# Loading a small decay vector through another engine's queue, and a new order of two early attention steps, in a fused attention and MLP kernel

## The chip, the cores and the metric

The kernel runs on one core of one Trainium2 chip. The metric is the device time of one execution in microseconds (us). A profile gives the span of one execution, from the first to the last instruction; the device time is about 1.8 us longer than the span. The experiments ran on three chips (e and g on one, f on another, h1 on a third), each with the kernel before beside it, so kernels of different letters are compared by their ratios to before.

In the profile PE is TensorE's matmuls, PEld its weight loads, DVE is VectorE, ACT is ScalarE, POOL is GpSimd, and SP is SyncE, whose work here is to issue transfers (SPq). ACTq is a transfer issued by ScalarE. PSUM is the memory that TensorE writes its results to; to evacuate a result is to copy it from there. A load has landed when all of its 16 completions have come.

## The reference

Decayed causal attention in blocks of 64 rows, then a two-layer MLP on its output.

```python
# q, k, v: (4 batches, 8 heads, 768 rows, 64);  lam: 8 decays, one per head
for b in range(nb):                                    # 12 blocks of 64 rows
    intra = einsum('bhic,bhjc->bhij', qb, kb) * Dmask  # lam ** (i - j), causal
    intra = einsum('bhij,bhjd->bhid', intra, vb)
    inter = einsum('bhid,bhde->bhie', qb * lam ** (pos + 1), kv_state)
    out[block] = intra + inter
    kv_state = lam ** 64 * kv_state + einsum('bhsd,bhse->bhde', kb * lam ** (63 - pos), vb)
x = out as (3072, 512)
result = gelu_tanh(x @ w_in) @ w_out                   # w_in 512 x 2048, w_out 2048 x 512
```

## The kernel before

The attention is cut into 24 steps, each of one batch, 256 rows and four of the eight heads. Steps 0 to 3 give the first 512 rows of x, and these start the MLP: its first group of work, `Hps = w_in . x` with GELU, then fills TensorE between the later attention steps. Every q, k, v and weight tile is loaded through SyncE's queue, in this order, with lam in front:

```python
    lam_bc = const.tile([P, H], FP32)
    pin(nc.sync.dma_start(out=lam_bc[:], in_=lam.unsqueeze(0).to_broadcast([P, H])))
    for s in range(4):
        load_step(s)                       # q, k, v of a step: three transfers of 256 KB
    for j in range(4):
        for part in ((0, 1) if j < 2 else (None,)):
            load_win(j, part)
    for j in (0, 2, 1, 3):
        load_wout(j)
    for s in range(4, 9):
        load_step(s)
```

One step passes through these stages: `prep` (q times a power of lam on VectorE, for step 3 on GpSimd; k cast on ScalarE, v on GpSimd), `stage_t` (eight transposes on TensorE into PSUM, then an evacuation), `scores`, `causal` (VectorE multiplies the scores by the mask, 1.22 us), `products` (the key product and the value product into the two PSUM banks OK), `update` (VectorE adds the key product to the running state, "t"; GpSimd spreads it, "u"), and `x_out` (ScalarE evacuates x, two pieces of 0.38 us each). The order of these calls is the program order on every engine. The order of before from step 2 on:

```python
    update(1, 0)
    idle(3)                                # three filler matmuls
    scores(2)
    products(2, None)
    causal(2)
    prep_v(3)
    update(2, 0)
    update(1, 1)
    update(2, 1, "t")
    idle(2)
    stage_t(3)
    OK1 = products(None, 1, evacuate=False)[0]
    OK2 = products(None, 2, evacuate=False)[0]
    x_out(2, OK2)
    x_out(1, OK1)
    scores(3)
    banks = products(3, None)
    update(3, 0)
    c01, c23 = slice(0, 2), slice(2, 4)
    cast_win(0, 0, 256, 128, c01)
    cast_win(0, 256, 512, 256, c01, on_act=True)
    causal(3)
    queue_group(0)
    fill(4)                                # fill(n): the next n pieces of MLP work
    products(None, 3, banks)
    ...                                    # cut
    # later, before step 4:
    cast_wout(0, (POOL, POOL))
    for m in W_SUMS:                       # five sums of w_out parts on VectorE
        sum_wout(0, m, DVE)
    fill(8)
    cast_wout(2, (ACT, ACT))
    cast_wout(1, (POOL, ACT))
    cast_wout(3, (POOL, ACT))
    fill(9)
    prep(4)
    stage_t(4)
```

## Time and profile before

| | before |
|---|---|
| device time, median of 3 runs | 206.26 us (206.10 to 206.67) |
| span of the profiled execution | 204.3 us |
| PE busy | 196.8 us (96%) |
| VectorE, ScalarE, GpSimd busy | 71%, 53%, 34% |

TensorE is busy for 96% of the span. Of the 7.5 us that it does not work, 3.7 are in the first 20 us, where the attention steps wait for loads and for each other, and 3.8 follow the last matmul (200.53), while the result leaves the core. The lines of the slices, the chain and the timeline of this kernel stand in the prediction below, each with what it shows.

### The profile page before, as it was taken

What the parts mean: (1) busy time and instruction counts of PE and PEld (TensorE: products, weight loads), DVE (VectorE), ACT (ScalarE), POOL (GpSimd) and SP (SyncE); (2) the same over time, 40 slices, a digit from 0 to 9 for tenths busy, and PEclk for the clock granted to TensorE, in tenths of its full rate; (3) what the DMA queues carried; (4) which work ended last, traced back from release to release, by engine and by line L of the source; (5) the groups of instructions that cost most, each with busy time, mean ns of one, the idle gap of its engine ahead of it and who ended that gap; (6) DMA issues with size and microseconds to landing.
All of it is one profiled execution on the core that took longest, in us unless ns stands there. A gap on an engine that the chain in (4) does not pass through costs nothing.

```text
span 204.3 us, 5584 instructions
## 1 busy us (share of the span) xinstructions
PE 196.8 (96%) x2321; PEld 127.6 (62%) x2321; DVE 144.8 (71%) x271; ACT 107.7 (53%) x204; POOL 70.1 (34%) x80
## 2 busy tenths in 40 slices
PE   7888999999999999999999999999999999999992
PEld 2454644456875788654688654788554788545881
DVE  4887627867599999929997828996739673136552
ACT  2364678475683573477722477641576331577110
POOL 5595123646487750436134404314412100000000
PEclk9999999999999999999999999999999999999999
DMA  4999999999999999996449993647330003300014
GB/s 132 299 321 385 387 388 379 285 291 315 297 262 228 296 241 173 235 285 176 91 128 266 181 279 94 152 107 156 75 85 0 0 3 103 107 0 0 3 51 156
DMA packets 64074, 37.86 MB, mean 185 GB/s; under 512 B 17712, under 2 KB 59184, under 8 KB 64048
## 3 DMA queue, kind: packets, MB, share of 16 engines
q1 hardware_dynamic: 63760, 37.24, 68.1%
q8 instruction: 18, 0.29, 0.6%
q10 hardware_dynamic: 288, 0.26, 0.4%
q14 instruction: 8, 0.07, 0.1%
HBM read 27.27 MB, written 6.29 MB: 164 GB/s over the span
## 4 chain that ended last, share of the span: by engine, by line
PE 89%; DMA 3%; SPq 2%; ACT 1%; DVE 1%; issue 1%
PE Hps L401 37%; PE O2ps L416 10%; PE MB L470 8%; PE MA L470 7%; PE MD L470 7%; PE Sps L271 4%; PE MC L470 4%; PE Hps L515 4%; PE OK L329 3%; PE OK L320 3%; DMA k<-in_k_dram 3%; SPq L68 2%; PE OK L306 1%; PE Tps L242 1%; DVE t L366 1%
## 5 line engine op out<-in xcount | busy, mean ns | idle before, releaser
L401 PE MATMUL Hps<-xT,w_in 128*128 128x512 f16 (+1 forms) x416 | 79.1, 346 | 0.0
L405 ACT ACTIVATE gT<-Hps 128x512 f16<-128x512 f32 x88 | 52.1, 598 | 21.9 <-PE Hps L401 21.1
L401 PEld LDWEIGHTS <-w_in 128*128 128x128 f16 x416 | 40.2, 98 | 33.5
L373 POOL TENSOR_TENSOR u<-t,lumask 128x256 f16<-128x256 f32 x40 | 31.4, 792 | 80.6 <-DVE t L366 58.4
L446 DVE TENSOR_TENSOR gs<-gT 128x512 f16<-128x512 f16 (+1 forms) x70 | 36.6, 586 | 10.8 <-ACT gT L405 10.6
L280 DVE TENSOR_TENSOR PT<-Sps,mask 128x1024 f16<-128x1024 f32 x24 | 29.2, 1216 | 17.1 <-PE Sps L271 17.1
L470 PEld LDWEIGHTS <-gs 128*128 128x128 f16 x360 | 34.9, 98 | 4.0
L211 POOL TENSOR_TENSOR v<-v,dv 128x512 f16<-128x512 f32 x24 | 29.2, 1220 | 4.9 <-DMA v<-in_v_dram 4.8
L343 ACT ACTIVATE xT<-OK 128x256 f16<-128x256 f32 x48 | 18.2, 454 | 20.0 <-PE OK L329 14.3
L416 PE MATMUL O2ps<-w_out,gT 128*128 128x512 f16 x96 | 21.9, 379 | 0.0
L226 ACT ACTIVATE qk<-k 128x512 f16<-128x512 f32 x24 | 15.0, 626 | 9.3 <-DMA k<-in_k_dram 9.3
L221 DVE TENSOR_TENSOR qk<-q,dq 128x512 f16<-128x512 f32 x23 | 19.3, 841 | 0.0
L477 ACT ACTIVATE m<-MB 128x512 f32<-128x512 f32 x9 | 5.4, 597 | 25.4 <-PE MB L470 25.4
L470 PE MATMUL MA<-w_sum,gT 128*128 128x256 f16 x144 | 17.5, 273 | 0.1
L470 PE MATMUL MD<-w_sum,gs 128*128 128x256 f16 x136 | 17.5, 273 | 0.0
L470 PE MATMUL MB<-w_out,gs 128*128 128x256 f16 x144 | 17.2, 273 | 0.0
L366 DVE SCALAR_TENSOR_TENSOR t<-t,lamu,OK 128x64 f32<-128x64 f32 x64 | 14.5, 273 | 2.3 <-PE OK L306 1.1
L470 PEld LDWEIGHTS <-gT 128*128 128x128 f16 x144 | 14.0, 98 | 2.8 <-ACT gT L405 0.3
L416 PEld LDWEIGHTS <-gT 128*128 128x128 f16 x96 | 9.2, 98 | 9.9
L481 DVE TENSOR_TENSOR o<-MA,m 128x512 f32<-128x512 f32 x9 | 6.2, 688 | 12.3 <-ACT m L477 12.3
L271 PEld LDWEIGHTS <-qkT 64*64 64x64 f16 x384 | 6.2, 106 | 8.6 <-issue 4.2
L123 DVE TENSOR_TENSOR w_sum<-wo,wo 128x1024 f16<-128x1024 f32 x6 | 7.9, 1362 | 4.2 <-DMA wo<-in_moe_w_out_dram 4.2
(55 smaller groups left out, 168.8 us busy)
## 6 DMA issues: line engine op xcount, KB each, us to landing
q<-in_q_dram SPq DMA_DIRECT2D x24, 256.0 KB, 4.5
k<-in_k_dram SPq DMA_DIRECT2D x24, 256.0 KB, 4.9
v<-in_v_dram SPq DMA_DIRECT2D x24, 256.0 KB, 4.9
out_dram<-o SPq DMA_DIRECT2D x22, 256.0 KB, 4.1
wo<-in_moe_w_out_dram SPq DMA_DIRECT2D x4, 1024.0 KB, 9.2
wi<-in_moe_w_in_dram SPq DMA_DIRECT2D x4, 512.0 KB, 8.0
wi<-in_moe_w_in_dram SPq DMA_DIRECT2D x2, 1024.0 KB, 12.5
out_dram<-o SPq DMA_DIRECT2D x2, 128.0 KB, 1.9
```

The source lines that it names most:

```text
L211: pin(nc.gpsimd.tensor_tensor(wide(tv[:]), ld32[s][2][:], decay(dv, s), ALU.mult))
L221: pin(q_eng.tensor_tensor(wide(tq), q32[:], decay(dq, s), ALU.mult))
L226: pin(nc.scalar.activation(out=wide(tk), in_=k32[:], func=AF.Copy))
L280: pin(nc.vector.tensor_tensor(t[:].rearrange("p a b c d -> p (a b) (c d)"), Ss.pop(n)[:].rearrange("p a b c d -> p (a b) (c d)"), mask[:]. ...
L343: pin(nc.scalar.activation(out=dst[:, :, c * P : (c + 1) * P].rearrange("p hp (t j) -> p hp j t", j=2), in_=OK[c][:, 0:256].rearrange("p ( ...
L366: pin(nc.vector.scalar_tensor_tensor(t[:, hp, :], state[half][:, hp, :], lamu[:, 2 * half + hp : 2 * half + hp + 1], K[:, hp, :], ALU.mult ...
L373: pin(nc.gpsimd.tensor_tensor(u[:], state[half][:].unsqueeze(2).to_broadcast([P, 2, 2, D]), lumask[:, 2 * half : 2 * half + 2, :].unsqueez ...
L401: pin(nc.tensor.matmul(by_block(Hps[:, i, :]), w_in16[:, c, f * P : (f + 1) * P], x(c), start=(c == 0), stop=(c == NC - 1)))
L405: pin(nc.scalar.activation(out=dst, in_=Hps[:], func=AF.Gelu_apprx_tanh))
L416: pin(nc.tensor.matmul(O2[tau][0][:], gT[:, f % HF, f // HF, tau * P : (tau + 1) * P], w_out16[:, f, :], start=(n == 0), stop=(n == NF - 1)))
L446: pin(nc.vector.tensor_tensor(gsum[m][:, i, :], block(T0, F0, i), block(T1, F1, i), op))
L470: pin(nc.tensor.matmul(dst, lhsT, rhs, start=(i == 0), stop=(i == HF - 1), skip_group_check=True))
```

## The change

The intent: lam's transfer no longer stands at the head of SyncE's queue. ScalarE issues it, to four partitions only (0, 32, 64, 96), and one VectorE shuffle spreads it to all 128, so that q of step 0 is the first transfer of SyncE. And steps 2 and 3 run in an order that waits less on VectorE's updates and starts the first MLP matmuls with one half of x. In the diff, `...` marks what is cut.

```diff
-    lam_bc = const.tile([P, H], FP32)
-    pin(nc.sync.dma_start(out=lam_bc[:], in_=lam.unsqueeze(0).to_broadcast([P, H])))
+    lam_in = const.tile([P, H], FP32)
+    pin(nc.vector.memset(lam_in[:], 0.0))
+    pin(nc.scalar.dma_start(out=lam_in[0:P:32, :], in_=lam.unsqueeze(0).to_broadcast([4, H])))
...
+    lam_bc = const.tile([P, H], FP32)
+    pin(nc.vector.stream_shuffle(lam_bc[:], lam_in[:], [0] * 32))
...
-        if s == 2:                         # evacuation of the transposes: half ACT, half DVE
+        if s in (2, 3):
...
-    def x_out(s, OK):
+    def x_out(s, OK, second=None):         # the second half may go to VectorE
...
-            for fs, stages in ((range(4), (((0, 1), both, False), ((2, 3), b0, False),
-                                           ((2, 3), b1, True))),
+            for fs, stages in ((range(4), (((0, 1), b0, False), ((0, 1), b1, False),
+                                           ((2, 3), b0, False), ((2, 3), b1, True))),
...
-    idle(11)
+    idle(9)
...
     update(1, 0)
+    update(1, 1, "t")
     idle(3)
     scores(2)
     products(2, None)
+    update(2, 0)
     causal(2)
     prep_v(3)
-    update(2, 0)
-    update(1, 1)
+    update(1, 1, "u")
+    stage_t(3)
+    products(None, 1)
+    products(None, 2)
     update(2, 1, "t")
-    idle(2)
-    stage_t(3)
-    OK1 = products(None, 1, evacuate=False)[0]
-    OK2 = products(None, 2, evacuate=False)[0]
-    x_out(2, OK2)
-    x_out(1, OK1)
     scores(3)
     banks = products(3, None)
-    update(3, 0)
     c01, c23 = slice(0, 2), slice(2, 4)
     cast_win(0, 0, 256, 128, c01)
     cast_win(0, 256, 512, 256, c01, on_act=True)
+    update(3, 0)
     causal(3)
     queue_group(0)
-    fill(4)
-    products(None, 3, banks)
-    cast_win(0, 0, 512, 256, c23)
     fill(8)
+    cast_win(0, 0, 256, 256, c23, on_act=True)
+    cast_win(0, 256, 512, 256, c23)
+    fill(2)
+    products(None, 3, banks, evacuate=False)
+    x_out(3, banks[0], nc.vector)
+    fill(6)
+    update(3, 1, "t")
     cast_win(1, 0, 512, 256, c01)
-    update(3, 1, "t")
     cast_win(1, 0, 512, 256, c23)
```

More of the change, by code (lines that the diff above doesn't have):

```diff
@@ L244, in stage_t @@
         o = qkp.tile([P, 2, 2, 2, P], FP16, tag="qkT", name=f"qkT_{s}")
-        if s == 2:
+        if s in (2, 3):
             pin(nc.scalar.activation(out=o[:, 0], in_=Tps[:, 0], func=AF.Copy))
             pin(nc.vector.tensor_copy(out=o[:, 1], in_=Tps[:, 1]))
-        elif s in (1, 3, 5, 6):
+        elif s in (1, 5, 6):
             pin(nc.scalar.activation(out=o[:], in_=Tps[:], func=AF.Copy))
@@ L342, in x_out @@
         for c in range(2):
-            pin(nc.scalar.activation(
-                out=dst[:, :, c * P : (c + 1) * P].rearrange("p hp (t j) -> p hp j t", j=2),
-                in_=OK[c][:, 0:256].rearrange("p (hp j t) -> p hp j t", hp=2, j=2),
-                func=AF.Copy))
+            d = dst[:, :, c * P : (c + 1) * P].rearrange("p hp (t j) -> p hp j t", j=2)
+            o = OK[c][:, 0:256].rearrange("p (hp j t) -> p hp j t", hp=2, j=2)
+            if c == 1 and second is not None:
+                pin(second.tensor_copy(out=d, in_=o))
+            else:
+                pin(nc.scalar.activation(out=d, in_=o, func=AF.Copy))
     us = {}
@@ L510, in mm1_part @@
         def mm1_part(f, cs, blocks, last):
-            if cs[0] == 0:
+            opens = f not in first
+            if opens:
                 first[f] = ps_M.tile([P, N], FP32, tag="M", name="Hps")
@@ L516, in mm1_part @@
                                      w_in16[:, c, f * P : (f + 1) * P], x(c)[:, blocks],
-                                     start=(c == 0), stop=last and c == NC - 1,
+                                     start=opens and c == 0, stop=last and c == NC - 1,
                                      skip_group_check=True))
```

## The prediction

> **What bounds the kernel now.** I read the page's slices first, then the chain of waits in order of time, then the timeline of the first 45 us, then the DMA issues one by one. The slices:
>
> ```profile
> PE   7888999999999999999999999999999999999992
> DMA  4999999999999999996449993647330003300014
> ```
>
> Each digit is a slice of 5.1 us. TensorE is the bound from slice 5 (20 us) to the end, and the change takes no full-rate matmul away there. What it does in the first 20 us is therefore worth the time by which it lets the full TensorE stream start earlier, and only as far as that stream's inputs also come earlier. Over slices 2 to 8 the DMA engines are full too, so two things set the pace: the attention steps 0 to 3 that lead to the first GELU matmul, and the queue of loads.
>
> The chain of waits (start, us, what) through that stage:
>
> ```profile
> 0.74 0.39 SPq L127
> 1.13 0.06 issue
> 1.19 0.42 SPq L68
> ...
> 5.75 5.32 DMA k<-in_k_dram
> 11.09 0.63 ACT qk L226
> 11.72 0.65 ACT xT L343 x2
> 12.38 0.54 ACT qkT L246
> 12.94 0.43 DVE qkT L247
> ...
> 15.40 0.48 DVE t L366 x2
> 15.92 0.41 PE OK L320 x15
> ...
> 17.82 0.21 DVE w_in L107
> ...
> 18.08 0.60 PE Hps L515 x2
> 18.72 1.47 PE Hps L515 x6
> ...
> 20.87 5.23 PE Hps L515 x32
> ```
>
> The reader is to see three things. The chain starts with lam's issue at the head of SyncE's queue and runs down that queue to k of step 2. Between 13.9 and 17.8 it goes through VectorE updates which hold a PSUM bank that the product of step 2 wants (15.40 to 15.92), and a cast of w_in that comes late. The first eight matmuls of the GELU product take 2.07 us from 18.08, where eight at full rate take 1.73 (8 x 0.216), and 32 more follow at full rate, ending at 26.1.
>
> The second place is where the TensorE stream meets step 4 (timeline: start, us, engine, line, operation):
>
> ```profile
> 32.16 3.50 DVE L123 TENSOR_TENSOR w_sum<-wo,wo 128x1024 f16<-128x1024 f32 x3 [4.20 <-DMA wo<-in_moe_w_out_dram]
> ```
>
> ```profile
> 37.79 1.88 POOL L117 CAST w_out<-wo 128x1024 f16<-128x1024 f32 x1 [1.23 <-DMA wo<-in_moe_w_out_dram]
> 38.69 1.52 DVE L221 TENSOR_TENSOR qk<-q,dq 128x512 f16<-128x512 f32 x1
> 39.39 0.63 ACT L226 ACTIVATE qk<-k 128x512 f16<-128x512 f32 x1 [0.57 <-DMA k<-in_k_dram]
> 40.40 0.65 PEld L242 LDWEIGHTS <-qk 128*128 128x128 f16 x8
> 40.61 0.61 PE L242 MATMUL Tps<-ident,qk 128*128 128x128 f16 x8
> ```
>
> VectorE cannot begin the sums of w_out before wo has landed at 32.16. It works without a pause (3.50, then 3.19 us for the other two) into q of step 4, which ends at 38.69 + 1.52 = 40.21. TensorE loads it at 40.40. TensorE shows no pause there now, but after VectorE's usual hand-over of some 0.05 us only about 0.14 us are left.
>
> **What the Trainium skill says.** "DMA: Bandwidth & Descriptors", section "Issuing engines are not separate DMA queues": DMAs of all issuers run on the same 16 engines, and a second issuer saves only sequencer time. The trace agrees that it is such time that can be saved: lam's issue takes 0.39 us and q's follows at 1.19. The page does not promise bandwidth, and from 4 us on I see none to gain (285 to 315 GB/s while q, k and v arrive, about 385 for the weights). "PSUM — Partial Sum Buffer", section "PSUM bank collisions raise a hardware error": two engines must not touch one bank in the same quadrant at once, reads included. The trace agrees: ACT's half of step 2's evacuation runs 12.30 to 12.90 and VectorE's half only starts at 12.94. "SBUF — State Buffer", terms, on the shared port pair of VectorE and GpSimd: the loser blocks. The trace agrees as far as it goes: q of step 4 took 1.52 us beside GpSimd's cast, where q of step 1 took 0.69 with GpSimd idle. "TensorE: Matmul & The Clock Gate", Part 1, says that full rate comes after a window of about 3.4 us of activity; here eleven warm-up matmuls take 4.87 us (0.44 each) and those after 6.6 us take about 0.22.
>
> **The change part by part.**
> (1) lam off the SyncE queue. q of step 0 issues at 0.74 instead of 1.19: 0.45 us. The queue is the head of one stream that goes on filled to 38 us (q, k, v of steps 0 to 3, w_in, w_out, q and k of step 4), so I move every landing in it by the same D. D is at least about 0.45; 128 small packets less in front may add up to 0.2. I use D = 0.5. Landings before, from issue plus time to landing: k0 5.45, k1 8.4, k2 11.05, k3 13.75, first half of the first w_in tile 17.2, its second half about 18.5.
> (2) lam itself. A memset of VectorE (0.07) precedes its issue by ScalarE, at about 1.0. If it lands after 2.2 us, as small ScalarE writes do at the end of this kernel, that is 3.2 instead of 3.74; the shuffle adds some 0.15 (my guess; an 8-wide multiply takes 0.17). GpSimd's power takes 1.01, the odd column 0.16, q0's product 0.69: q0 ready near 5.4, before it was 5.74. k0, cast at 4.95 to 5.6, stays the later one. So lam is not on the path; its queue slot was.
> (3) The new order of step 2 and 3. On VectorE two updates (2 x 0.47) now precede the mask of step 2 (1.22), which ends near 15.2 instead of 15.1, though the loads are earlier. In exchange the banks are free when the products of steps 1 and 2 ask for them: no 0.17 us wait at 15.92. The split evacuation of step 3 costs 0.60 + 0.42 one after the other, against 1.02 on ScalarE alone: nothing. Products of step 1 then run 14.5 to 15.2, of step 2 15.3 to 16.0, scores and key products of step 3 to 16.75 (before: 17.35).
> (4) First GELU matmuls by block. They need only the first block of x, so they wait on w_in alone: landing 17.2 - 0.5 = 16.7, one cast of 128 columns 0.33, start at 17.05 instead of 18.08. 16 matmuls of 256 columns take 16 x 0.108 = 1.73, to 18.9; two of the next stage 0.43; product of step 3 0.7, its mask ending by then at 19.05; the other twelve matmuls 1.3 with some 0.1 of waiting for x of step 3. Total: 21.45. Then 16 of 512 columns, 3.46, end at 24.9. Before: 26.1. So the front gains about 1.2 us.
> (5) Two warm-up matmuls fewer: TensorE waits there anyway, nothing.
>
> How much of 1.2 survives: the inputs of step 4 move only by D. VectorE's sums, GpSimd's cast and q4 are all released by landings, so q4 is ready at 40.26 - 0.5, and the stream, which comes 1.2 early to 40.40, waits 1.2 - 0.5 - 0.14 = about 0.55 us there. What remains is D + 0.14 = 0.64 us. The other late inputs have more slack: k4 ends at 40.02 and is wanted near 40.8; w_out parts are wanted 2 us after their landing or more. After step 4 TensorE has no pause but about 0.3 us at 77 us, which hangs on ScalarE's own order and moves along. Sum: 206.26 - 0.64 = 205.6.
>
> **The rivals.** A: the front's 1.2 us arrive whole, because VectorE and GpSimd meet differently at 38 us and q4 takes nearer 0.7 than 1.52; then 205.0 to 205.1. Against it: both are released by the same stream. B: lam comes late, since ScalarE's table load (1.28 us, from 0.73) might stand before the issue; lam would land near 4.2, q0 at 6.3, and steps 0 and 1 lose 0.5. The front has 0.55 to spare before that costs anything, so 205.6 to 206.1. C: the stream is bound by bytes from the start, and lam's slot was hidden: D = 0 to 0.1, then only 0.2 is left: 206.0. Against it: in 2.6 to 3.2 us the engines are only partly busy (0.62 to 0.84) and the first landings follow the issues. D: the later mask of step 2 or a wait for a PSUM bank, with six in the pool and four opened at once by the new order, eats the front's gain: 206.2 to 206.6. Nothing before shows such a wait after 16 us, but its order is the one that I cannot see.
>
> **Range and chances.** Main line 205.6, A pulls down by half a us, B to D up by half a us: 205.0 to 206.2. Two per cent is 4.1 us; all the TensorE idle time before 20 us, with its warm-up matmuls, holds that, but the loads don't allow it. Faster by over 2%: 0.01; within: 0.98; slower: 0.01.
>
> **What would show it.** k0, k1, k2 landing 0.45 to 0.65 earlier (step 1); q0 ready before k0 (2); no VectorE update in front of the product of step 2 (3); first GELU matmul near 17.1 and the end of the first group at about 24.9 (4); a TensorE wait of some 0.5 us for q of step 4 near 39.7, and from there a constant lead of 0.6 us to the end. I am wrong if landings do not move, if no wait shows at step 4 and the lead at 60 us is over 1 us, or if the first GELU matmul starts after 17.8.

## The result and the profile after

The first comparison gave 205.02 us for the changed kernel (median of 4 runs, 204.98 to 205.40) against 206.44 us for the kernel before (206.10 to 206.67), a ratio of 0.9937 [0.9917, 0.9957]. A ratio in this text is the mean time of one kernel's fast runs over that of the other's of the same rounds, so it is not quite the ratio of the medians quoted; the brackets are its 95% interval. Two repeats, told below, gave 0.9974 and 0.9957. Over the sixteen executions of the three comparisons the mean of the changed kernel is 205.47 us, some 0.9 us under before.

The slices of the profiled execution after (5.1 us each):

```profile
PE   7788999999999999999999999999999999999993
DMA  5999999999999999996669993648330003300014
```

At this scale almost nothing has changed; slice 2 of PE is a step lower, since there are fewer filler matmuls. The difference has to be read at landmarks of the stream. The table has them for every kernel, in us from the start of the span, as the trace of one execution each has them; the kernels with a letter and number are the experiments below. "w_in" is the landing of the first w_in part, "group end" is the first full-rate MLP matmul after the first group of `Hps`, "step 4" is the start of the transposes of step 4, "last product" is the start of the last eight matmuls, and "end" is the time from there to the end of the span.

```
                   w_in    group end  step 4   last product  end    span
before             17.21   25.93      40.61    199.49        4.84   204.33
before, g1         17.16   26.44      41.12    199.98        4.86   204.84
after              16.83   25.12      39.89    198.76        4.44   203.20
after, e1          16.91   25.35      40.03    198.88        4.44   203.32
after, g2          16.69   25.06      40.10    198.97        4.43   203.41
e2 lam only        15.54   25.76      40.44    199.29        4.44   203.73
e3 order only      17.25   25.54      40.31    199.18        4.86   204.04
f1 lam by SyncE    17.67   25.95      40.72    199.59        4.84   204.43
f2 11 warm-ups     17.05   25.33      40.11    198.97        4.44   203.41
f3 one more load   17.21   25.50      40.39    199.26        4.76   204.02
e4 q4 free         16.99   25.28      39.96    198.82        4.44   203.26
f4 both edits      16.29   24.77      39.44    198.30        4.44   202.74
g3 both, 11        17.04   25.06      40.17    199.03        4.46   203.49
h1 both but sums   16.16   24.71      39.39    198.45        4.44   202.89
```

(In e2 w_in landed earliest of all, but its old order does not wait for it: it casts w_in at 17.56, after an update.) The trace of after leads that of before by 0.81 us at the end of the first group, 0.72 at step 4 and 0.73 at the last product. Then it gains another 0.40 after the last product, which makes 1.13 of span. So there are three places to explain: the front, step 4 and the end.

**The front.** The chain of waits of the kernel after up to the first full-rate matmul (start, us, what):

```profile
0.74 0.45 SPq L68
...
4.79 1.50 SPq L68
...
9.88 6.95 DMA wi<-in_moe_w_in_dram
...
16.86 0.31 DVE w_in L107
...
17.21 2.36 PE Hps L522 x20
...
20.28 0.46 DVE xT L350
...
20.78 4.50 PE Hps L522 x24
```

Before, the chain left the queue at k of step 2 and went on through the attention steps, with VectorE's updates in it. Now it stays in SyncE's queue until w_in lands at 16.83, and the attention steps are beside it. The update wait at 15.92 of before is gone. What follows w_in is one cast, the first 20 matmuls in 2.36 us (20 at full rate would take 2.16), the evacuation of x of step 3, and 24 matmuls after it.

The timeline of the same kernel at the start (start, us, engine, line, operation, and in brackets the idle time before it and what ended it):

```profile
0.91 1.09 ACTq L129 DMA_DIRECT2D lam_in<-in_lam_dram  x1
2.03 1.28 ACT L169 ACT_TABLE_LOAD   x1 [2.03 <-DVE lumask L165]
3.90 0.17 DVE L167 STREAM_SHUFFLE lam_bc<-lam_in 128x8 f32<-128x8 f32 x1
4.60 0.63 ACT L230 ACTIVATE qk<-k 128x512 f16<-128x512 f32 x1 [1.07 <-DMA k<-in_k_dram]
5.42 0.69 DVE L225 TENSOR_TENSOR qk<-q,dq 128x512 f16<-128x512 f32 x1
```

lam itself is later than before (3.88 against 3.74), since ScalarE takes 1.09 us to issue it. q of step 0 is ready at 6.11 us, after k of step 0, which was cast by 5.23; before, k was the later of the two. This costs nothing, because step 1's loads set the pace: its transposes start at 8.45 us, before at 8.63.

The loads do not all move by the 0.45 us of the queue slot. k of step 0 lands 0.88 us earlier (4.58 against 5.46), but k of steps 1, 2 and 3 only 0.28 (8.09, 10.79 and 13.50 against 8.37, 11.07 and 13.79), and w_in 0.38. In the view of one stretch (start and end, us, then busy time of PE, PEld, DVE, ACT and POOL with counts, the granted clock, the mean busy share of the DMA engines, GB/s), before:

```profile
4.00:5.00 1.00, 1.00 (x4) 0.43 (x3) 0.75 (x5) 0.00 (x0) 1.00 (x2) 1.00 1.04 306
```

and after:

```profile
4.00:5.00 1.00, 1.00 (x4) 0.30 (x2) 0.83 (x6) 0.40 (x1) 0.84 (x1) 1.00 0.83 235
```

The DMA engines moved 235 GB/s instead of 306 in that microsecond, and 212 instead of 285 in the next. Three of the 16 completions of v of step 0 came at 6.10 to 6.28 us, the others at 4.95 to 5.56. Why those three lagged the trace does not show. So in this pair two thirds of the 0.88 us did not reach the loads behind.

But one pair misleads here, since landings scatter and those of k in before are the earliest of their kind. In the other two traces with lam's 128 packets at the head (g1 and e3 below) k of step 1 landed at 9.03 and 8.71; in the ten with lam on ScalarE it landed at 7.92 to 8.41. By the means of these three and ten traces k of step 0 lands 1.01 us earlier and k of steps 1, 2 and 3 0.51 to 0.52 us earlier. The first part of w_in scatters more, because one of its 16 completions lags: in before 15 had come by 15.99 and the last came at 17.21, in after by 15.64 and at 16.83. In the ten traces the 15th came at 15.36 to 15.89, the last at 15.54 to 17.21. Most of the spread in the column of w_in is this one completion.

**Step 4.** The timeline of after where the stream meets step 4:

```profile
38.31 1.52 DVE L225 TENSOR_TENSOR qk<-q,dq 128x512 f16<-128x512 f32 x1
39.88 0.45 PEld L246 LDWEIGHTS <-qk 128*128 128x128 f16 x8 [0.42 <-DVE qk L225]
39.89 0.62 PE L246 MATMUL Tps<-ident,qk 128*128 128x128 f16 x8
```

The weight load now waits 0.42 us for q of step 4, where in before it showed no wait. But only 0.09 of it becomes a loss of lead.

**The end.** From the last product on, before:

```profile
199.49 1.04 PE L470 MATMUL ME<-w_sum,gs 128*128 128x256 f16 x8
...
201.01 0.36 SPq L499 DMA_DIRECT2D out_dram<-o  x1
```

and after:

```profile
198.76 1.04 PE L476 MATMUL ME<-w_sum,gs 128*128 128x256 f16 x8
...
200.29 0.36 SPq L505 DMA_DIRECT2D out_dram<-o  x1
```

From the last product to the last issue both kernels take the same, 1.52 and 1.53 us. The 0.40 us are in what follows: from that issue to the end of the span it is 3.32 us before and 2.91 after. The prediction had nothing on this.

### The profile page after: what moved, and what is told of

The parts are those of the page before. It is cut to its first block, busy times and chain, and to the rows that moved or that the text cites. A ratio compares the mean times of both kernels' runs of the same rounds, so it can differ in the third digit from the quotient of the medians.

```text
span 203.2 us, 5595 instructions
## 1 busy us (share of the span) xinstructions
PE 195.5 (96%) x2325; PEld 127.4 (63%) x2325; DVE 144.8 (71%) x275; ACT 108.2 (53%) x204; POOL 70.1 (34%) x80
## 4 chain that ended last, share of the span: by engine, by line
PE 89%; SPq 4%; DMA 3%; issue 1%; DVE 1%; ACT 1%
PE Hps L407 37%; PE O2ps L422 10%; PE MB L476 8%; PE MA L476 7%; PE MD L476 7%; SPq L68 4%; PE MC L476 4%; PE Sps L275 3%; DMA wi<-in_moe_w_in_dram 3%; PE Hps L522 3%; PE OK L333 3%; PE OK L324 3%; PE Tps L246 1%; PE OK L310 1%; PE ME L476 0%
## 5 line engine op out<-in xcount | busy, mean ns | idle before, releaser
L352 ACT ACTIVATE xT<-OK 128x256 f16<-128x256 f32 x47 | 18.0, 453 | 18.9 <-PE OK L333 15.3
```

The costliest lines, as they stand in the source:

```text
L352: pin(nc.scalar.activation(out=d, in_=o, func=AF.Copy))
```

## The experiments

My theory after this reading: the change gains by two parts that add up, the queue slot (through the landing of w_in) and the order (which makes the start of the MLP depend on that landing alone); q of step 4 takes back a little; and the end of the program is shorter because SyncE issues one transfer less. The rivals: one part does everything; the queue slot matters for its bytes and not for its time; the end is shorter by chance; the gain at the front comes from the warm-up matmuls.

### Is the result repeatable? (e1, g2, g1)

No edit: the changed kernel twice more, and the kernel before against itself.

> The changed kernel once more, unedited, for a second trace and more times. Theory 1 (the lead is cut by a late q of step 4): TensorE again starts step 4's transposes 0.7 us before the kernel before (39.9 against 40.6), and the time is 0.7 us lower plus or minus what differs between executions, ratio 0.995 to 0.997. Theory 2 (the gain is the 1.3 us of the first comparison, and 0.4 to 0.6 us of it arise at the end of the program or outside the TensorE stream): ratio 0.993 to 0.995, and the tail between the last VectorE addition and the end of the span is again shorter by 0.3 to 0.4 us. Also: k of step 0 lands 0.9 us earlier but k of step 1 only 0.3; if that is the order of issue, it repeats; if a stray slow DMA engine, k1 is 0.3 to 0.9 earlier.

Measured: 205.91 us (205.10 to 206.77, 6 runs) against 206.40, ratio 0.9974 [0.9952, 0.9996].

> The changed kernel, unedited, a third time: lead at the last product 0.6 to 0.75 us, end of program 4.44 us, so 1.0 to 1.15 us less in the trace; ratio 0.994 to 0.997, with some executions 0.8 us or more above the fastest if the spread is its own.

Measured: 205.14 us (204.75 to 206.16) against 206.26, ratio 0.9957 [0.9936, 0.9978].

> The kernel before, unedited, for a second trace. From the start of the last product's matmuls to the end of the span it takes 4.84 us again (4.44 in every trace without lam's load on the SyncE queue), step 4's transposes start near 40.6 and w_in's first part is cast from 17.7; ratio 1.000.

Measured: 206.32 us (205.94 to 206.82), ratio 1.0002 [0.9985, 1.0019].

The gain is there each time, and its size differs between comparisons by more than a factor of two (0.0026 to 0.0063 of the time). Some executions of the changed kernel are 0.8 to 1.7 us over its fastest (in e1 four of six, up to 206.77 against 205.10); before itself spreads by 0.9 us within the six of g1 and by 1.5 us over the eleven in the same rounds. No profiled execution fell among the slow ones, so what lengthens them is open.

The traces say more on the front. The two of before differ: w_in landed at the same time (17.21 and 17.16), yet the group ended at 25.93 and 26.44. The old order depends on its own attention chain (k of step 1 landed at 8.37 in the first and at 9.03 in the second). The three of after end the group 8.29, 8.44 and 8.37 us after w_in lands. TensorE reached full rate at 5.62 us in the first and at 7.17 us in e1 without much effect.

### One part at a time (e2, e3)

e2 is the kernel before with lam's part alone:

```diff
 # before.py
-    lam_bc = const.tile([P, H], FP32)
-    pin(nc.sync.dma_start(out=lam_bc[:], in_=lam.unsqueeze(0).to_broadcast([P, H])))
+    lam_in = const.tile([P, H], FP32)
+    pin(nc.vector.memset(lam_in[:], 0.0))
+    pin(nc.scalar.dma_start(out=lam_in[0:P:32, :], in_=lam.unsqueeze(0).to_broadcast([4, H])))
...
+    lam_bc = const.tile([P, H], FP32)
+    pin(nc.vector.stream_shuffle(lam_bc[:], lam_in[:], [0] * 32))
```

> The kernel before with lam's load and shuffle alone changed. Theory 1: the landings move by the 0.3 us seen after, the old order passes this on and no more; first GELU matmul 17.7 to 17.8 (before 18.08), lead of 0.3 us at step 4, less than the slack there, so nothing is cut: about -0.3 us, ratio 0.9985. Rival (the queue slot is the whole change): -0.7 or more, ratio 0.9966 or below. Rival (lam later means q0 later means nothing gained): 0.

Measured: 205.88 us (205.44 to 206.52) against 206.40, ratio 0.9978 [0.9961, 0.9995]; group end 25.76, end 4.44. The old order's wait for an update is still in its timeline:

```profile
15.90 0.41 PE L324 MATMUL OK<-PT,v 64*64 64x128 f16 x15 [0.17 <-DVE t L370]
```

e3 is the kernel after with lam loaded as before, so the order alone:

```diff
 # after.py
-    lam_in = const.tile([P, H], FP32)
-    pin(nc.vector.memset(lam_in[:], 0.0))
-    pin(nc.scalar.dma_start(out=lam_in[0:P:32, :], in_=lam.unsqueeze(0).to_broadcast([4, H])))
+    lam_bc = const.tile([P, H], FP32)
+    pin(nc.sync.dma_start(out=lam_bc[:], in_=lam.unsqueeze(0).to_broadcast([P, H])))
...
-    lam_bc = const.tile([P, H], FP32)
-    pin(nc.vector.stream_shuffle(lam_bc[:], lam_in[:], [0] * 32))
```

> The changed kernel with lam again at the head of the SyncE queue and no shuffle. Theory 1: landings as before, so the first GELU matmul waits for w_in at 17.2 plus the cast, 17.5, and the end of its first group comes 0.5 us earlier than before; q of step 4 is at its old 40.2, and TensorE can come at most some 0.33 us earlier to it: -0.33 us, ratio 0.9984. Rival (no cut at step 4): -0.5 us, ratio 0.9976. Rival (the reorder does nothing): 0.

Measured: 205.81 us (205.72 to 205.99) against 206.40, ratio 0.9973 [0.9961, 0.9986]; w_in at 17.25, group end 25.54, end 4.86.

Both parts gain, some 0.45 us (0.0022 of 206.4) and 0.56 us (0.0027). The sum of 1.0 us is close to the 0.9 us of the whole change over its sixteen executions. But in the same rounds the whole change (e1) gave 0.9974, no more than either part, so the times alone do not show that the parts add up. The spans of the traces fit it better: 0.60 and 0.29 us below before, and 1.13, 1.01 and 0.92 for the three traces of the whole. What they gain differs in kind. lam's part leads at the last product by 0.20 us only and has the other 0.40 at the end; the order leads by 0.31 and has nothing at the end. In e3 w_in lands where it did before, and the group ends 8.29 us later, as in after: the order gains without any earlier load.

### What of lam's transfer costs: its time in the queue or its packets? (f1)

f1 keeps the load to four partitions and the shuffle, but lets SyncE issue it again at the head:

```diff
 # after.py
-    pin(nc.scalar.dma_start(out=lam_in[0:P:32, :], in_=lam.unsqueeze(0).to_broadcast([4, H])))
+    pin(nc.sync.dma_start(out=lam_in[0:P:32, :], in_=lam.unsqueeze(0).to_broadcast([4, H])))
```

> The changed kernel, but lam's small load of four partitions is issued at the head of the SyncE queue; the shuffle stays. If the queue slot is what counts: landings of q, k, v as in the kernel before, lead of TensorE at step 4 about 0.3 us as in the run with the new order alone, end of program (from the last SyncE wait on the output to the end of the span) 1.55 us as before: -0.3 us, ratio 0.9985. If the 128 small packets counted: landings of k0 0.3 us or more earlier than before, lead 0.6 or more. If ScalarE's queue is what makes the times of the changed kernel spread (205.0 to 206.8), these executions lie within 0.3 us.

Measured: 206.50 us (206.03 to 207.94) against 206.19, ratio 1.0020 [0.9996, 1.0044]: nothing gained, although the order's part is in it. Its timeline:

```profile
0.90 0.71 SPq L129 DMA_DIRECT2D lam_in<-in_lam_dram  x1
1.67 0.42 SPq L68 DMA_DIRECT2D q<-in_q_dram  x1
```

The transfer has 4 packets instead of 128, yet its issue took 0.71 us instead of 0.39, and waited for VectorE's memset until 0.90. q of step 0 was issued at 1.67, 0.48 later than before. It landed at 4.64 all the same, as before, and k of step 0 shows it too. Its cast starts as it lands, first in before, then in f1:

```profile
5.48 0.63 ACT L226 ACTIVATE qk<-k 128x512 f16<-128x512 f32 x1 [2.81 <-DMA k<-in_k_dram]
5.52 0.63 ACT L230 ACTIVATE qk<-k 128x512 f16<-128x512 f32 x1 [2.86 <-DMA k<-in_k_dram]
```

From issue to landing q of step 0 took 3.45 to 3.52 us behind the 128 packets (before, g1, e3), 2.97 behind the four of f1, and 2.95 to 3.04 with lam on ScalarE (ten traces). In before lam's packets ran until 3.36 us, among the first of q. So the packets cost the first loads about as much as the slot, 0.46 and 0.45 us, which is why k of step 0 gained 0.88. Later loads of f1 lie where those of before, g1 and e3 do (k of step 1 at 8.75, of step 3 at 14.15). Only the last completion of w_in was late, at 17.67; the group ended 8.28 us after it, so in this trace the gain of the order was just used up. f1 therefore does not show that the slot alone counts. Why its other executions are slower still is open.

### Does one SyncE transfer more lengthen the end? (f3)

f3 issues a second, unread load of lam behind the first loads, where nothing waits for it:

```diff
 # after.py, behind the loads of steps 4 to 8
+    lam_again = const.tile([P, H], FP32)
+    pin(nc.sync.dma_start(out=lam_again[0:P:32, :], in_=lam.unsqueeze(0).to_broadcast([4, H])))
```

> The changed kernel with one more tiny load on the SyncE queue, after the first loads, into a tile that nobody reads: SyncE's program has as many DMA issues again as before. Theory (the shorter end of the program, 1.14 against 1.55 us from the last wait to the end, hangs on the length of SyncE's program): the end takes 1.5 to 1.6 us again, TensorE's last matmul as in the changed kernel, time 0.3 to 0.4 us above the changed kernel. Rival (chance, or lam on ScalarE's queue itself): the end stays at 1.1 to 1.2.

Measured: 205.74 us (205.54 to 206.47) against 206.19, ratio 0.9981 [0.9966, 0.9995]. The end is 4.76 us, against 4.43 to 4.46 in all nine traces of kernels without a lam load on SyncE (after, e1, g2, e2, e4, f2, f4, g3, h1) and 4.84 to 4.86 in all four with one at the head (before, g1, e3, f1). So a transfer that nobody waits for brings back 0.32 of the 0.40 us: the end depends on what SyncE's program holds, not on the order. In the traces two of SyncE's closing DRAIN instructions start 0.39 us apart in before, 0.37 in f3 and 0.06 in after. How SyncE's program sets that is open. w_in also landed later in f3 (17.21), although the extra load comes behind it; I count that to the lagging completion (15 had come by 15.89).

### Do the warm-up matmuls matter? (f2)

```diff
 # after.py
-    idle(9)
+    idle(11)
```

> The changed kernel with eleven warm-up matmuls instead of nine. If the spread of the changed kernel's times comes from TensorE reaching its full rate late in some executions (at 7.2 us in the second trace of it, 5.6 in the first), the executions now lie within 0.4 us and near 205.0. If it comes from the DMA rings, the spread stays (0.8 us or more between the fastest and the slowest).

Measured: 205.19 us (204.98 to 205.67) against 206.19, ratio 0.9950 [0.9938, 0.9962]. w_in landed at 17.05 and the group ended 8.28 us after it, as with nine. The two warm-ups are neutral in the trace, as predicted. The executions lie closer together than in e1 or g2, but e2 and g3, which also have eleven, each had an execution at least 0.9 us over their fastest (206.52 and 206.12), so whether the warm-ups bear on the spread is not settled. TensorE was granted its full clock at 4.16 to 7.17 us in the eight traces with nine warm-ups and at 4.41 to 7.48 in the six with eleven, which shows no difference.

### Is it q of step 4 that takes back lead? (e4)

e4 gives the last w_out cast of GpSimd to VectorE and lets the one sum that needs only the first w_out tile go first, so that q of step 4 runs while GpSimd is idle:

```diff
 # after.py
-                pin(nc.gpsimd.tensor_copy(out=dst, in_=src))
+                pin(eng[i].tensor_copy(out=dst, in_=src))
...
-    for m in W_SUMS:
+    for m in (6, 3, 4, 1, 7):
...
-    cast_wout(3, (POOL, ACT))
+    cast_wout(3, (DVE, ACT))
```

> The changed kernel, with q of step 4 made early: GpSimd's half of the last w_out cast goes to VectorE [...] and the sum that needs one w_out tile alone goes first. Theory 1: q4 takes about 0.7 us instead of 1.52 and ends near 38.9, no TensorE wait at step 4, the lead of 0.82 us from the first group is kept whole: 0.1 us below the changed kernel, no more, because the first group then is the limit. Rival (the cut at step 4 hides more than 0.1): 0.3 us or more below it. Rival (VectorE is now too full there): no better or worse.

Measured: 205.00 us (204.77 to 206.21) against 206.40, ratio 0.9942 [0.9922, 0.9962]. The timeline at step 4:

```profile
38.42 0.69 DVE L225 TENSOR_TENSOR qk<-q,dq 128x512 f16<-128x512 f32 x1
...
39.96 0.61 PE L246 MATMUL Tps<-ident,qk 128*128 128x128 f16 x8
```

q of step 4 takes 0.69 us instead of 1.52 and is ready 0.85 us before TensorE uses it. That agrees with what the Trainium skill's "SBUF — State Buffer", section Terms, says of the port pair that VectorE and GpSimd share: the loser of the two waits. e4 changes the sums too, but h1 below, which keeps their order, has 0.68. The lead is 0.65 us at the group end and 0.65 at step 4, so nothing is lost. In after 0.81 became 0.72. The third trace of after shows the wait reaching the matmuls when the lead is a little larger:

```profile
40.10 0.62 PE L246 MATMUL Tps<-ident,qk 128*128 128x128 f16 x8 [0.20 <-DVE qk L225]
```

There 0.87 at the group end became 0.51. In e1 the lead against before's first trace is 0.58 both times, in e3 0.39 became 0.30. Of the seven traces with the new order and the old q of step 4, six lose 0.09 to 0.36 us here, and in these the transposes start 0.05 or 0.06 us after q ends; e1 loses nothing. So the wait exists, and the edit removes it. How much it takes is not set by the lead alone: f3 lost 0.21 of 0.43. The time of e4 is level with after's within the intervals, because its front was no better in that execution than after's (w_in 16.99).

### A faster front and a free q4 (f4, g3, h1)

The new order puts the value product of step 3 behind 20 matmuls; four more do not need its x, and then TensorE waits for VectorE's evacuation (20.28 in the chain above). f4 moves the value product of step 3 two pieces forward, behind 16 matmuls, on top of e4:

```diff
 # e4
-    fill(2)
     products(None, 3, banks, evacuate=False)
     x_out(3, banks[0], nc.vector)
-    fill(6)
+    fill(8)
```

> The run with q of step 4 freed, and in addition the product of step 3 two matmul groups earlier, so that eight instead of six groups cover the evacuation of x of step 3. If the front is what now limits: first group's end 0.2 to 0.25 us earlier for the same landing of w_in, no wait before the second block's matmuls, and the time 0.2 us below the run with q4 freed. If the cut at step 4 or the landings limit: no gain.

Measured: 205.01 us (204.52 to 206.47) against 206.19, ratio 0.9946 [0.9922, 0.9970]. The lead is 1.16 us at the group end and 1.17 at step 4: again no cut. But most of the 1.16 is not the edit's: w_in landed at 16.29, half a us earlier than in after, and no line that the edit touches comes before that landing. From landing to group end it took 8.48 us.

g3 is f4 with eleven warm-up matmuls:

```diff
 # f4
-    idle(9)
+    idle(11)
```

> The changed kernel with q of step 4 freed, the product of step 3 earlier and eleven warm-up matmuls. If the parts add up: lead 0.9 to 1.2 us, end 4.44, 1.3 to 1.6 us below the kernel before and 0.2 to 0.5 below the changed kernel; if the eleven warm-ups matter, no execution more than 0.8 us above the fastest, where the same with nine had one.

Measured: 205.08 us (204.80 to 206.12) against 206.26, ratio 0.9950 [0.9930, 0.9969]. Here w_in landed at 17.04 and the group ended 8.02 us later, 0.26 to 0.42 less than in the kernels with after's order: with a late w_in the edit does gain. But 0.87 of lead became 0.44 at step 4, and not through q:

```profile
29.71 3.07 POOL L117 CAST w_out<-wo 128x1024 f16<-128x1024 f32 x2 [8.05 <-DMA wo<-in_moe_w_out_dram]
32.84 0.59 PE L422 MATMUL O2ps<-w_out,gT 128*128 128x512 f16 x2 [0.27 <-POOL w_out L117]
```

The sum that now comes first runs beside GpSimd's two casts, which take 3.07 us instead of 2.02, and TensorE waits for the second. The cure for one wait had put another in its place.

h1 therefore takes g3 without the new order of the sums:

```diff
 # g3
-    for m in (6, 3, 4, 1, 7):
+    for m in W_SUMS:
```

> As the run of the parts together, but without the sum put first, which in that run slowed GpSimd's first w_out cast to 3.07 us and made TensorE wait for it. Expected: no wait at step 4 (q4 takes 0.7 us and ends near 39.1), none at the first w_out product, lead at the last product as large as at the end of the first group, 0.8 to 1.1 us; ratio 0.993 to 0.995. If the lead is again smaller at the last product than at the end of the first group, another landing cuts it.

Measured: 204.83 us (204.66 to 205.03) against 206.20, ratio 0.9936 [0.9922, 0.9949]. At step 4 and before:

```profile
19.51 5.36 PE L522 MATMUL Hps<-xT,w_in 128*128 128x256 f16 x32
...
38.59 0.68 DVE L225 TENSOR_TENSOR qk<-q,dq 128x512 f16<-128x512 f32 x1
...
39.39 0.61 PE L246 MATMUL Tps<-ident,qk 128*128 128x128 f16 x8
```

The 32 matmuls from 19.51 run without a wait for x, q of step 4 takes 0.68 us, the group ends 8.55 us after w_in lands, and the lead of 1.22 at the group end is still 1.22 at step 4 (0.18 of it is lost between there and the last product, which I did not follow up). w_in had landed early in this execution (16.16), so not all of that lead is the edit's. h1 has the lowest median of all and the closest executions, and beats the kernel before; against the changed kernel, with ratios of 0.9937, 0.9957 and 0.9974 and on other chips, an advantage is likely but not proven.

## Why the prediction was right

The prediction was 205.6 us (205.0 to 206.2), with 0.98 for within 2%. The first comparison gave 205.02, at the lower edge of the range; the mean of sixteen executions, 205.47, is near its middle. Part of that is luck, as the steps show.

**Step 1, every landing moves by D = 0.5.** Right behind the first loads, on the average of the traces; the first pair alone (0.28) hid it. Between the three traces with lam's 128 packets at the head (before, g1, e3) and the ten with lam on ScalarE, k of steps 1, 2 and 3 moves by 0.51, 0.52 and 0.51 us and w_in by 0.54 (17.21 to 16.67; 0.41 without e2, the only one with the old order). w_in scatters by more than that. It did not move the stream as one: k of step 0 gained 1.01. The prediction gave the packets at most 0.2; f1 shows 0.48 at q of step 0 (3.45 to 2.97). Rival C (D of 0 to 0.1, the slot hidden behind bytes) falls with these means, and not with f1.

**Step 2, lam not on the path.** The conclusion held and the reasoning did not. lam landed at 3.88 and not at 3.2, q of step 0 was ready at 6.11 and not near 5.4, and it came after k of step 0. Rival B had nearly the right times (4.2 for lam, 6.3 for q of step 0) but not the right cause: the table load came after the issue, at 2.03; the issue itself took 1.09 us. Its lateness was harmless because step 1's landings gate.

**Step 3, no update wait at the products.** Right: the mask of step 2 ended at 15.45 (predicted 15.2), and the wait of 0.17 us for an update is gone in after and present in e2. In its place stands a wait of 0.33 us for that mask at 15.50, beside the load of w_in, so it cost nothing. No run separates the split evacuation of step 3. Rival D fell: the chain of after shows no wait for a PSUM bank.

**Step 4, the first MLP matmuls wait on w_in alone.** Right in mechanism: in the eight traces with after's order of the fills (after, e1, g2, f2, f3, e4, e3, f1) the group ends 8.28 to 8.44 us after w_in lands, whatever the attention did before; with the old order it was 8.72, 9.28 and, in e2, 10.22. The size was off: the group was to end at 24.9 and ended, read from the chain as the prediction did, at 25.28. Of these 0.38 us, 0.13 is the landing (16.83, not 16.7). Another 0.18 is the wait for VectorE's evacuation of x of step 3, put at 0.1: after the product, at 20.25, the last 28 matmuls took 5.03 us, where full rate takes 4.75, so TensorE waited about 0.28. The first 20 matmuls took 2.36 us and not 2.16, but a slip in the prediction's sum (17.05 + 1.73 is 18.78, not 18.9) hid 0.12 of that. So the front gained 0.81 and not 1.2.

**Step 5, two warm-ups fewer do nothing.** Right in the traces (f2).

**The cut at step 4.** q of step 4 is what stops the lead, as e4 shows by removing it, so the mechanism was right; its size was predicted as 0.55 and measured as 0.09 in after, 0 in e1 and 0.36 in the third trace of after. In after the front had brought less to cut. And the slack was taken as 0.14 us, from the end of q to the weight load at 40.40; the gap from that load to the first matmul at 40.61 was slack as well, since in after the matmuls start 0.01 us after the load (39.88 and 39.89). With a landing shift of 0.38 and slack of 0.14 + 0.20 = 0.34 the lead can be 0.72, which is what the trace has.

**The sum.** "What remains is D + 0.14 = 0.64 us" against 0.73 at the last product: the front too large by 0.39 and the cut too large by 0.46 almost cancel.

**What the prediction missed** is the end: 0.40 us that come with one SyncE transfer less. It is 0.40 of the 1.13 us by which the trace of after is shorter, and without it the first comparison would have lain near 205.4, well inside the range rather than at its lower edge.

## What to carry to other kernels

When a stream that must not stop is released by a load, make its first instructions depend on that load alone, and read the gain from landing to first full-rate work; the old order here lost 0.4 to 1.9 us between the two. A small load at the head of a load queue costs the first loads behind it its issue time and, where it is many packets, their time as well (0.45 and 0.46 us here), so move it away or make it few packets, but see how long its issue takes. Compare landings over several traces, since one pair here showed 0.28 us where the mean is 0.51. A lead won early lasts only to the next input that is not earlier, so look there for the wait, and check that curing it (a sum moved beside a GpSimd cast) makes no new one.

## What the Trainium skill lacked or had wrong

- "DMA: Bandwidth & Descriptors", section "Issuing engines are not separate DMA queues": it says rightly that another issuer saves only the time of issue. It lacks what that time depends on. Here lam's load took 0.39 us to issue from SyncE to 128 partitions, 0.71 us from SyncE to 4 partitions, and 1.09 us from ScalarE to 4 partitions.
- The same page says why small descriptors are slow, but has no figure for what they cost the load behind them in the queue. Here q of step 0 landed 3.45 to 3.52 us after its issue behind lam's 128 packets, 2.97 behind four, and 2.95 to 3.04 with lam on ScalarE.
- "Runtime: NRT & Kernel Launch" lists stages that follow the kernel, but no page that I found says what makes the end of the profiled program longer: from the last product to the end of the span it took 4.43 to 4.46 us without a lam transfer on SyncE's queue, 4.84 to 4.86 with one at its head and 4.76 with one further back that nothing waits for.
